# The last product's second tile in two 128-column halves, with its store cut in two

## The chip, the cores and the metric

The kernel runs on one core of one Trainium2 chip. Its time is the device time of one execution in microseconds (us); all times here are in us unless marked ns. The engines are TensorE (PE; its weight loads are shown apart as PEld), VectorE (DVE), ScalarE (ACT), GpSimd (POOL) and SyncE (SP). SP, ACT and POOL also issue DMA transfers, each on a queue of its own (SPq, ACTq, POOLq in the profile), and 16 DMA engines move the bytes.

## The reference

The inputs are `x` (8 batches, 8 heads, 512 rows, 64 columns), `state` (8 batches, 8 heads, 32 rows, 64 columns), `w_in` (512 x 2048) and `w_out` (2048 x 512), all float32.

```python
scores = scale * x @ state^T;  a  = softmax(scores);  xread = a @ state
scores2 = scale * state @ x^T; a2 = softmax(scores2); sread = a2 @ x
rows = concat([xread, sread], axis=2)      # (8, 8, 544, 64)
rows = rows.transpose(0, 2, 1, 3).reshape(8 * 544, 8 * 64)
h = rows @ w_in
out = max(0.01 * h, h) @ w_out             # (4352, 512) float32
```

So each batch gives 512 rows of `out` from `xread` and behind them 32 rows from `sread`: batch b's sread rows are rows 544 b + 512 to 544 b + 543.

## The kernel before, in words

Partitions are the 128 lanes of the on-chip memory; a tile is [partitions, columns]. The kernel works batch by batch. For a batch it computes attention, folds `state` and `w_in` into one matrix M, gets the hidden layer hT (2048 hidden units in 16 blocks of 128 partitions, 512 rows as columns) by `ff1`, and then the product with `w_out`. That product is done with seven half-size products in place of eight, Strassen's way: `product(b, n, v)` is the n-th of the seven for the row tile v (128 of 256 rows), eight matmuls which add up in one PSUM bank. The products 1, 6, 7 and 4 add up in the banks called "x", the products 2, 5 and 3 in those called "b". `after(b, n)` takes the intermediate sums out (`keep`, `y_add`) and stores them (`y_pair`). For the last batch, b = 7, the "x" sums of the two row tiles lie in a bank each (tiles `ppw`).

The order of the work on every engine is that of the program text (a manual schedule): an engine or a queue takes its instructions in that order, and each waits for what it needs. So an instruction that waits holds up all behind it on the same engine or queue.

At the start TensorE runs matmuls on an idle tile (`spin`), between the first real ones. They write to a bank that nobody reads.

The end of the program goes as follows. The sread rows of all eight batches, 256 rows, go through the two layers together: `f_product` is the first layer, `two_product(q, n)` the second, again in seven products, and `q.y` holds the result, 128 partitions by two halves u, of 512 columns each. Half u holds four batches of 32 rows. After product 3 half u = 0 is done and goes out from SP, after product 4 half u = 1 from ACT, in four stores of 64 KB each (line 1284), one per batch. Meanwhile the last batch's own products lie between: products 2, 5, 6 and 7 between the `f_product` calls, product 3 behind the sread rows, and product 4 as the last work of the program (lines 1287 to 1294):

```python
for v in range(2):
    product(b, 4, v)
    (VEC, SCA)[v](y_block(b, 1, 0)[:, v], prods[b]["x"][v])
    nc.sync.dma_start(rows_of(b)[2 + v][:, :HN], y_block(b, 1, 0)[:, v])
```

VEC is a copy on DVE, SCA one on ACT. `y_block(b, 1, 0)[:, v]` is a 128 x 256 part of a tile in SBUF (HN = 256, P = 128); `rows_of(b)[2 + v]` are every fourth row of the batch, from row 2 + v on, so that each of these two stores takes 128 rows of 1 KB. Before them, `y_pair(b, 0, HN, DM)` stores two row tiles at once (256 KB in rows of 1 KB, line 745).

After the last store SP waits for every transfer that is still under way; then all engines meet, and the program ends.

Of the kernel before, what the change touches and what calls it, by code (L numbers as in the profile page):

```python
# [9 lines left out]
P = 128  # L10
B, H, S, D = 8, 8, 512, 64
NS = 32
DFF = 2048
DM = 512
SROW = S + NS
NT = S // P
NK = H // 2
# [3 lines left out]
FP32 = mybir.dt.float32  # L21
AF = mybir.ActivationFunctionType
ALU = mybir.AluOpType
# [4 lines left out]
def kernel(  # L28
# [9 lines left out]
    nc = tc.nc  # L38

    consts = ctx.enter_context(tc.tile_pool(name="consts", bufs=1))  # L40
# [6 lines left out]
    psum = ctx.enter_context(tc.tile_pool(name="psum", bufs=2, space=bass.MemoryType.PSUM))  # L47
# [5 lines left out]
    VEC, SCA, POO = nc.vector.tensor_copy, nc.scalar.copy, nc.gpsimd.tensor_copy  # L53
# [83 lines left out]
    def cast_x0(q, copy):  # L137
        v = q % 2
        copy(
            xs[0][q // 2][:, :, 2 * v:2 * v + 2].rearrange("p t h d -> p h t d"),  # L140
            xf[q][:].rearrange("p h (t d) -> p h t d", t=NT),
        )
# [15 lines left out]
    def spin_bank():  # L158
        return psum.tile([P, S], FP32, name="pspin", tag="py")

    def spin(p, n, w=S):
        for _ in range(n):
            nc.tensor.matmul(p[:, :w], lhsT=idle[:, :P], rhs=idle[:, :w], start=True, stop=True)
# [26 lines left out]
    def st1_evict():  # L190
        SCA(
            st1[:].rearrange("p (k q r) -> p k q r", k=NK, r=4),
            pst[:, :, D:].rearrange("p r (k q) -> p k q r", q=8),
        )
# [365 lines left out]
    HN = DM // 2  # L560
# [13 lines left out]
    def w_block(r, c, j0, j1):  # L574
        return w_out_bf[:, HJ * r + j0:HJ * r + j1, HN * c:HN * (c + 1)]
# [12 lines left out]
    hTs, sums, prods = {}, {}, {}  # L588
# [20 lines left out]
    def w_of(n, j):  # L609
        if n < 4:  # L610
            r, c = {1: (0, 0), 2: (1, 0), 3: (1, 1)}[n]
            return w_block(r, c, j, j + 1)[:, 0]
        return tw[{4: 4, 5: 1, 6: 2, 7: 3}[n]][j // 4][:, j % 4]

    def product(b, n, v, j0=0, j1=8):
        q = prods.setdefault(b, {})
        bank = "x" if n in (1, 6, 7, 4) else "b"
        first = n in (1, 2, 5) and v == 0 and j0 == 0
        if first:
            if b == B - 1 and n == 1:  # L620
                ts = [psum.tile([P, 2, DM], FP32, name="ppw", tag=t, bufs=1) for t in ("sc", "big")]
                q[bank] = [t[:, 0, :HN] for t in ts]
                q["whole", bank] = None
            else:
                t = psum.tile([P, 2, HN], FP32, name=f"pp{bank}", tag="py")
                q[bank] = [t[:, u] for u in range(2)]
                q["whole", bank] = t[:]
        wide = b == B - 1 and n == 1
        q["open", bank] = first or (wide and j0 == 0)
        at = slice(P * v, P * (v + 1))  # L630
        low = slice(HN * 1 + P * v, HN * 1 + P * (v + 1))
        for j in range(j0, j1):
            lhsT = {
                1: lambda: hTs[b][:, j, at],
                2: lambda: hTs[b][:, HJ + j, at],
                4: lambda: hTs[b][:, HJ + j, low],
                3: lambda: sums[b, 4][:, j, at],
                5: lambda: sums[b, 1][:, j, at],
                6: lambda: sums[b, 2][:, j, at],
                7: lambda: sums[b, 3][:, j, at],  # L640
            }[n]()
            nc.tensor.matmul(  # L642
                q[bank][v], lhsT=lhsT, rhs=w_of(n, j), start=q["open", bank] and j == 0,
                stop=j == 7, skip_group_check=True,
            )

# [71 lines left out]
    def keep(b, n):  # L718
        q = prods[b]
        if n == 5:  # L720
            t = consts.tile([P, 2, HN], FP32, name="s5", tag="stf4")
        else:
            t = ypool.tile([P, 2, HN], FP32, name=f"s{n}", tag=f"s{n}", bufs=1)
        q[n] = t
        for to, of in bank_parts(q, "b" if n == 5 else "x", t[:]):
            SCA(to, of)

    def y_block(b, u, c):
        q = prods[b]
        if ("y", u) not in q:  # L730
            q["y", u] = ypool.tile([P, 2, DM], FP32, name="ysb", tag="ysb")
        return q["y", u][:, :, HN * c:HN * (c + 1)]

    def y_add(b, u, c, bank, n):
        q = prods[b]
        kept = q[n][:]
        for v, (to, of) in enumerate(bank_parts(q, bank, y_block(b, u, c))):
            in1 = kept if q["whole", bank] is not None else kept[:, v]
            nc.vector.tensor_tensor(out=to, in0=of, in1=in1, op=ALU.add)  # L739
# [4 lines left out]
    def y_pair(b, u, c0=0, c1=DM):  # L744
        nc.sync.dma_start(
            pair_rows(b, u)[:, :, c0:c1],
            prods[b]["y", u][:, :, c0:c1],
        )

    def after(b, n):  # L750
        if n == 1:
            keep(b, 1)
        elif n == 2:
            y_add(b, 0, 0, "b", 1)
        elif n == 6:
            keep(b, 6)
        elif n == 5:
            keep(b, 5)
        elif n == 7:
            y_add(b, 1, 1, "x", 5)  # L760
        elif n == 3:
            y_add(b, 0, 1, "b", 6)
            y_pair(b, 0)
        elif n == 4:
            SCA(y_block(b, 1, 0), prods[b]["whole", "x"])
            y_pair(b, 1)

    def rows_of(b):
        return out[b * SROW:b * SROW + S, :].rearrange("(p t) f -> t p f", t=NT)
# [11 lines left out]
    def x0_t(q):  # L781
        ps = psum.tile([P, NT, P], FP32, name="pxth", tag=("ph", "py")[q // 2])
        for t in range(NT):
            nc.tensor.matmul(
                ps[:, t, :], lhsT=pair_of(a0, t, q), rhs=ident[:], start=True, stop=True
            )
        SCA(a0.xT[:, :, q, :], ps[:])
# [3 lines left out]
    def scores0(q):  # L791
        if q < 2:
            if q == 0:
                sct["low"] = psum.tile([P, 2, NT, 2, NS], FP32, name="sct", tag="sc", bufs=1)
            sct[q] = sct["low"][:, q]
        else:
            t = psum.tile([P, NT, 2, NS], FP32, name="sct", tag=("big", "py")[q - 2], bufs=q - 1)
            sct[q] = t[:]
        for t in range(NT):
            nc.tensor.matmul(  # L800
                sct[q][:, t].rearrange("p c n -> p (c n)"),
                lhsT=a0.xT[:, t, q, :], rhs=stbd[:, q].rearrange("p g n -> p (g n)"),
                start=True, stop=True,
            )

    scn, e10, r0, qb0 = {}, {}, {}, {}
# [82 lines left out]
    for q in range(2):  # L889
        cast_x0(q, VEC)  # L890
        x0_t(q)
        if q == 0:
            st1_evict()
            bank = spin_bank()
            spin(bank, 3, S // 2)
    spin(bank, 2, S // 2)
    scores0(0)
    cast_x0(2, VEC)
    x0_t(2)
    spin(bank, 2, S // 2)  # L900
    scores0(1)
    cast_x0(3, VEC)
    x0_t(3)
    bank = spin_bank()
# [3 lines left out]
    scores0(2)  # L908
    max0(2)
    rows0(0)  # L910
    spin(bank, 2, S // 2)
    scores0(3)
    max0(3)
    spread0(scn[0], m, False)
# [5 lines left out]
    q = [recip0(0)]  # L920
# [331 lines left out]
    b = B - 1  # L1252
    for c in range(2):
        f = f_open(c)
        for n, own in (
            (1, ()), (2, ((2, 5)[c], 0)), (6, ()), (5, ((2, 5)[c], 1)),
            (7, ()), (3, ((6, 7)[c], 0)), (4, ((6, 7)[c], 1)),
        ):
            f_product(f, n)
            if own:  # L1260
                product(b, *own)
                if own[1]:
                    after(b, own[0])
            if c == 0 and n == 2:
                for m in (1, 2):
                    s_sum(b, m, 4, 8, nc.vector)
                for j in range(0, HJ, 2):
                    s_sum(b, 4, j, j + 2, nc.gpsimd)
        if c == 0:
            y_pair(b, 0, 0, HN)  # L1270
            q = two_open(hs, 0, None, "ph")
            for n in range(1, 5):
                two_sum(q, n, 0, 4, nc.vector)
# [4 lines left out]
    for n in (1, 2, 6, 5, 7, 3, 4):  # L1278
        two_product(q, n)
        if n in (3, 4):  # L1280
            u = n - 3
            for v in range(NK):
                r0 = (NK * u + v) * SROW + S
                (nc.sync, nc.scalar)[u].dma_start(
                    out[r0:r0 + NS, :], q.y[NS * v:NS * (v + 1), u]
                )
    for v in range(2):
        product(b, 3, v)
    y_add(b, 0, 1, "b", 6)
    y_pair(b, 0, HN, DM)  # L1290
    for v in range(2):
        product(b, 4, v)
        (VEC, SCA)[v](y_block(b, 1, 0)[:, v], prods[b]["x"][v])
        nc.sync.dma_start(rows_of(b)[2 + v][:, :HN], y_block(b, 1, 0)[:, v])


# [28 lines left out]
```

## Time and profile before

| what | us |
|---|---|
| median of three runs (lowest, highest) | 202.45 (202.29, 202.52) |
| the profiled execution | 202.64 |
| its span, first to last instruction | 200.9 |
| TensorE busy | 193.9 (97% of the span) |
| DVE, ACT, POOL busy | 158.7, 142.0, 72.9 |
| granted TensorE clock, mean over the span | 0.997 of full speed |
| bytes moved by DMA | 27.75 MB, 138 GB/s on the mean |

The profile is of one execution. Its views that are used here: the chain of work that ended last (followed back from the last instruction, at each step to what released it); the timeline (instructions in order of time, each with its start, its length, the engine, the line, and in brackets the engine's idle time before it with what ended it); the answers for one line (shortest, median and longest duration, first and last start, and for a DMA the time from issue to landing); and windows (busy time of each engine in a stretch, the granted clock, the mean busy share of the 16 DMA engines and the GB/s they moved). "out<-in" names tiles; `x16` counts instructions. Releasers are inferred from the times of events, so two events that fall together can be taken for each other.

### The profile page before, as it was taken

Reading aid. Unit: us, or ns where it says so; the run is one execution under the profiler, and the core shown is the slowest. Engines: PE = TensorE matmul, PEld = TensorE weight load, DVE = VectorE, ACT = ScalarE, POOL = GpSimd, SP = SyncE. Lnnn points to the kernel's source line nnn. Section 1 sums busy time; section 2 is a strip of 40 time slices with the busy share of each in tenths; the row PEclk is TensorE's granted clock in tenths of the full one; section 3 lists DMA queues with packets and bytes.
Section 4 is the critical chain, followed back from the end, with each engine's and each line's share of the span. In section 5 each row is a group of like instructions: output and inputs, shape, how many; then the busy total and the mean of one; then the engine's idle time right before and its main releaser. Section 6 shows DMA issues by size and latency. Waiting matters only on the chain.

```text
span 200.9 us, 4601 instructions
## 1 busy us (share of the span) xinstructions
PE 193.9 (97%) x1853; PEld 130.2 (65%) x1880; DVE 158.7 (79%) x241; ACT 142.0 (71%) x274; POOL 72.9 (36%) x76
## 2 busy tenths in 40 slices
PE   7899999999999999999999999999999999999993
PEld 3653444343476767776776677676767777799982
DVE  2665798589999989985999889898999945984712
ACT  3679747999889868766877779777868555757420
POOL 8834173991091373037300760054004600540000
PEclk9999999999999999999999999999999999999998
DMA  5999999697999844952473404220025202210115
GB/s 191 202 206 291 217 274 176 124 337 170 204 222 223 312 45 37 277 211 55 90 223 144 123 18 89 104 109 0 0 107 157 53 3 104 108 50 7 52 39 170
DMA packets 38773, 27.75 MB, mean 138 GB/s; under 512 B 24416, under 2 KB 35808, under 8 KB 38752
## 3 DMA queue, kind: packets, MB, share of 16 engines
q1 hardware_dynamic: 33584, 20.78, 39.9%
q0 software_dynamic: 4832, 6.29, 15.5%
q10 hardware_dynamic: 336, 0.39, 0.8%
q8 instruction: 14, 0.23, 0.5%
q14 instruction: 7, 0.06, 0.1%
HBM read 17.30 MB, written 8.91 MB: 131 GB/s over the span
## 4 chain that ended last, share of the span: by engine, by line
PE 77%; DMA 16%; POOL 3%; ACT 2%; issue 1%; ACTq 1%; SPq 0%; POOLq 0%
PE ph L442 21%; PE ppx L642 18%; PE ppb L642 15%; DMA xl<-in_x_dram 7%; DMA w_out_bf<-in_moe_w_out_dram 6%; PE ppr L699 6%; PE py L547 3%; PE pm L421 3%; PE pf L520 3%; PE ppw L642 3%; PE psr L394 2%; POOL w_in_bf L145 2%; DMA st_t<-stb 1%; DMA out_dram<-ysb 1%; PE sc L256 1%
## 5 line engine op out<-in xcount | busy, mean ns | idle before, releaser
L447 ACT ACTIVATE hT<-ph 128x512 bf16<-128x512 f32 x112 | 66.5, 604 | 25.1 <-PE ph L442 22.0
L607 POOL TENSOR_TENSOR S<-hT,S 128x512 bf16<-128x512 bf16 x24 | 32.1, 1358 | 82.2 <-DVE S L607 55.5
L442 PE MATMUL ph<-aT,M 128*128 128x512 bf16 x202 | 60.7, 379 | 0.1
L642 PEld LDWEIGHTS <-S 128*128 128x128 bf16 x384 | 37.0, 98 | 12.7 <-issue 0.9
L642 PEld LDWEIGHTS <-hT 128*128 128x128 bf16 x288 | 28.0, 98 | 11.1
L607 DVE TENSOR_TENSOR S<-hT 128x1024 bf16<-128x1024 bf16 x24 | 25.0, 1069 | 3.4 <-ACT hT L447 3.3
L442 PEld LDWEIGHTS <-M 128*128 128x128 bf16 x224 | 20.9, 98 | 8.7 <-issue 2.7
L642 PE MATMUL ppx<-tw,S 128*128 128x256 bf16 x160 | 20.8, 273 | 0.3
L547 PEld LDWEIGHTS <-hT 128*128 128x128 bf16 x96 | 9.1, 98 | 11.4 <-issue 1.0
L547 PE MATMUL py<-w_out_bf,hT 128*128 128x512 bf16 x61 | 15.6, 379 | 0.1
L739 DVE TENSOR_TENSOR ysb<-ppb,s 128x512 f32<-128x512 f32 x12 | 8.3, 692 | 6.2 <-PE ppb L642 6.2
L642 PE MATMUL ppb<-w_out_bf,hT 128*128 128x256 bf16 x96 | 12.4, 273 | 0.2
L642 PE MATMUL ppb<-tw,S 128*128 128x256 bf16 x96 | 12.4, 273 | 0.1
L642 PE MATMUL ppb<-w_out_bf,S 128*128 128x256 bf16 x96 | 12.3, 273 | 0.2
L435 ACT CAST M<-pm 128x1024 bf16<-128x1024 f32 x11 | 11.2, 1018 | 0.5 <-PE pm L421 0.5
L642 PE MATMUL ppx<-w_out_bf,hT 128*128 128x256 bf16 x80 | 11.2, 272 | 0.1
L347 ACT ACTIVATE e<-sc,mcol 128x512 bf16<-128x512 f32 x16 | 11.1, 701 | 0.0
L586 POOL TENSOR_TENSOR tw<-w_out_bf 128x512 bf16<-128x512 bf16 x8 | 9.0, 1154 | 4.5 <-DMA w_out_bf<-in_moe_w_out_dram 4.5
L642 PE MATMUL ppx<-tw,hT 128*128 128x256 bf16 x80 | 10.4, 273 | 0.2
L341 DVE TENSOR_REDUCE mcol<-sc 128x2 f32<-128x1024 f32 x8 | 9.7, 1214 | 0.0
L266 DVE TRANSPOSE_TENSOR_REDUCE mrow<-sc 128x32 f32<-128x1024 f32 x7 | 8.7, 1241 | 1.2 <-PE sc L256 1.2
L289 DVE TRANSPOSE_TENSOR_REDUCE r<-e 128x32 f32<-128x1024 bf16 x7 | 8.7, 1244 | 1.1 <-ACT e L330 0.8
(148 smaller groups left out, 323.7 us busy)
## 6 DMA issues: line engine op xcount, KB each, us to landing
out_dram<-ysb SPq DMA_DIRECT2D x11, 512.0 KB, 2.6
xl<-in_x_dram SPq DMA_DIRECT2D x5, 1024.0 KB, 6.0
out_dram<-ysb SPq DMA_DIRECT2D x9, 256.0 KB, 4.5
w_in_bf<-in_moe_w_in_dram POOLq DMA_DIRECT2D x4, 512.0 KB, 9.6
xf<-in_x_dram SPq DMA_DIRECT2D x4, 256.0 KB, 4.0
w_out_bf<-in_moe_w_out_dram POOLq DMA_DIRECT2D x4, 256.0 KB, 14.1
x<-in_x_dram POOLq DMA_DIRECT2D x2, 512.0 KB, 14.1
w_out_bf<-in_moe_w_out_dram POOLq DMA_DIRECT2D x2, 512.0 KB, 16.0
```

The costliest lines, as they stand in the source:

```text
L266: nc.vector.tensor_reduce(out=m1[:], in_=flat.rearrange("p (c j) -> p c j", j=NS), axis=AX.X, op=ALU.max, apply_transpose=True,)
L289: nc.vector.tensor_reduce(out=r1[:], in_=e1[:].rearrange("p (c j) -> p c j", j=NS), axis=AX.X, op=ALU.add, apply_transpose=True,)
L341: nc.vector.tensor_reduce(out=a.m2[:], in_=a.sc[:], axis=AX.X, op=ALU.max, negate=True)
L347: nc.scalar.activation(out=a.e2[:, g], in_=a.sc[:, g, :], func=AF.Exp, bias=a.m2[:, g:g + 1], accum_out=a.r2[:, g:g + 1],)
L435: copy(a.M[:, :, cols], pm[:])
L442: nc.tensor.matmul(ph[:], lhsT=a.M[:, g, P * j:P * (j + 1)], rhs=a.aT[:, g, :], start=(g == 0), stop=(g == 1),)
L447: nc.scalar.activation(out=hT[:, j, :], in_=ph[:], func=AF.Prelu, scale=1 / SCALE, alpha=0.01)
L547: nc.tensor.matmul(y.py, lhsT=hT[:, j, P * i:P * (i + 1)], rhs=w_out_bf[:, j, :], start=(j == 0), stop=(j == 15),)
L586: eng.tensor_tensor(out=tw[n][u][:, at], in0=in0, in1=in1, op=ALU.subtract)
L607: eng.tensor_tensor(out=part(n), in0=in0, in1=in1, op=op)
L642: nc.tensor.matmul(q[bank][v], lhsT=lhsT, rhs=w_of(n, j), start=q["open", bank] and j == 0, stop=j == 7, skip_group_check=True,)
L699: nc.tensor.matmul(q.bank[w], lhsT=lhsT, rhs=w_of(n, j), start=n in (1, 2, 5) and j == 0, stop=j == HJ - 1, skip_group_check=True,)
```

## The change

There are four edits.

- The second row tile of product 4 is done in two halves of 128 columns: the first 128 columns in its bank as before, the other 128 in a fresh bank (`end`). As the fresh bank lacks the sum of products 1, 6 and 7, these 128 columns are copied by ACT into a tile `last` after product 7, and DVE adds them at the end. ACT copies the first half and stores it (64 KB) from its own queue; DVE's half is stored (64 KB) from SP.
- `product` gets the columns c0 to c1 and a bank to write to.
- The sread rows of half u = 0 go out in three stores in place of four: batches 0 and 1 alone (64 KB each), batches 2 and 3 together (128 KB). The target of the third is a block of two batches by 32 rows, with a stride of 544 rows between the batches; its source is 64 partitions.
- Of the spins between the first matmuls, nine of 256 columns become four of 512 and one of 256, at the same places.

```diff
-    def product(b, n, v, j0=0, j1=8):
+    def product(b, n, v, j0=0, j1=8, c0=0, c1=HN, bank_of=None):
...
             nc.tensor.matmul(
-                q[bank][v], lhsT=lhsT, rhs=w_of(n, j), start=q["open", bank] and j == 0,
+                q[bank][v][:, c0:c1] if bank_of is None else bank_of,
+                lhsT=lhsT, rhs=w_of(n, j)[:, c0:c1],
+                start=(q["open", bank] or bank_of is not None) and j == 0,
                 stop=j == 7, skip_group_check=True,
             )
...
             bank = spin_bank()
-            spin(bank, 3, S // 2)
-    spin(bank, 2, S // 2)
+            spin(bank, 1)
+            spin(bank, 1, S // 2)
+    spin(bank, 1)
...
-    spin(bank, 2, S // 2)
+    spin(bank, 1)
     scores0(1)
...
-    spin(bank, 2, S // 2)
+    spin(bank, 1)
     scores0(3)
...
                 if own[1]:
                     after(b, own[0])
+                if own == (7, 1):
+                    last = consts.tile([P, P], FP32, name="last", tag="stf2")
+                    SCA(last[:], prods[b]["x"][1][:, P:])
...
             u = n - 3
-            for v in range(NK):
-                r0 = (NK * u + v) * SROW + S
-                (nc.sync, nc.scalar)[u].dma_start(
-                    out[r0:r0 + NS, :], q.y[NS * v:NS * (v + 1), u]
-                )
+            rows = out.rearrange("(b s) f -> b s f", s=SROW)[NK * u:NK * (u + 1), S:]
+            for v0, v1 in ((0, 1), (1, 2), (2, 4)) if u == 0 else ((v, v + 1) for v in range(NK)):
+                (nc.sync, nc.scalar)[u].dma_start(rows[v0:v1], q.y[NS * v0:NS * v1, u])
...
-    for v in range(2):
-        product(b, 4, v)
-        (VEC, SCA)[v](y_block(b, 1, 0)[:, v], prods[b]["x"][v])
-        nc.sync.dma_start(rows_of(b)[2 + v][:, :HN], y_block(b, 1, 0)[:, v])
+    y = y_block(b, 1, 0)
+    product(b, 4, 0)
+    VEC(y[:, 0], prods[b]["x"][0])
+    nc.sync.dma_start(rows_of(b)[2][:, :HN], y[:, 0])
+    end = psum.tile([P, P], FP32, name="end", tag="ph")
+    product(b, 4, 1, c1=P)
+    SCA(y[:, 1, :P], prods[b]["x"][1][:, :P])
+    nc.scalar.dma_start(rows_of(b)[3][:, :P], y[:, 1, :P])
+    product(b, 4, 1, c0=P, bank_of=end[:])
+    nc.vector.tensor_tensor(out=y[:, 1, P:], in0=end[:], in1=last[:], op=ALU.add)
+    nc.sync.dma_start(rows_of(b)[3][:, P:HN], y[:, 1, P:])
```

## The prediction

> **What bounds the kernel now.** I read the page's chain first, then the chain of the last stretch in order of time, then that stretch's timeline, and last the DMA views of the same stretch.
>
> ```profile
> span 200.9 us, 4601 instructions
> ...
> PE 77%; DMA 16%; POOL 3%; ACT 2%; issue 1%; ACTq 1%; SPq 0%; POOLq 0%
> ```
>
> TensorE carries the span from some 39 us on. The edits lie where it does not: in the first 9 us and behind its last products.
>
> ```profile
> 194.19 0.02 issue
> 194.21 0.38 ACT ysb L706
> ...
> 196.04 1.68 DMA out_dram<-ysb
> 197.72 0.35 ACT ysb L1293
> ```
>
> This chain, taken from 190 us on, says that ACT's last copy (L1293) was released by a store. It was not: as built, that copy waits for TensorE alone, and the store's landing fell 0.02 us beside TensorE's end. The timeline shows it:
>
> ```profile
> 193.79 1.76 SPq L1284 DMA_DIRECT2D out_dram<-ysb  x4
> ...
> 194.61 1.88 ACTq L1284 DMA_DIRECT2D out_dram<-ysb  x4
> ...
> 195.76 1.91 PE L642 MATMUL ppw<-tw,hT 128*128 128x256 bf16 x16
> 195.96 0.69 DVE L739 TENSOR_TENSOR ysb<-ppb,s 128x512 f32<-128x512 f32 x1 [2.19 <-PE ppb L642]
> 196.68 0.39 SPq L745 DMA_DIRECT2D out_dram<-ysb  x1
> 196.83 0.42 DVE L1293 COPY ysb<-ppw 128x256 f32<-128x256 f32 x1 [0.18 <-PE ppw L642]
> 197.28 1.16 SPq L1294 DMA_DIRECT2D out_dram<-ysb  x2
> 197.70 0.37 ACT L1293 COPY ysb<-ppw 128x256 f32<-128x256 f32 x1 [3.12 <-DMA out_dram<-ysb]
> ```
>
> TensorE ends at 195.76 + 1.91 = 197.67, ACT's copy at 198.07, the last issue starts at 198.10. Next, what the stores of lines 1294 and 1284 take from issue to landing:
>
> ```profile
> L1294 SPq DMA_DIRECT2D out_dram<-ysb x2: 345/350/356, 197.3 to 198.1; - x2
> ...
> DMA to landing us min/median/max: 1.8/2.0/2.2
> ```
>
> ```profile
> L1284 SPq DMA_DIRECT2D out_dram<-ysb x4: 350/414/432, 193.8 to 195.1; - x4
> L1284 ACTq DMA_DIRECT2D out_dram<-ysb x4: 395/444/473, 194.6 to 196.0; - x4
> ...
> DMA to landing us min/median/max: 1.6/1.8/2.1
> ```
>
> The last store took 1.84 (the minimum of its line): 199.94. The remaining 0.93 of the span is closing work, unchanged. Last, four windows: the sread stores; the final stores; one 256 KB store in rows of 1 KB alone; one 512 KB store in rows of 4 KB alone.
>
> ```profile
> 194.60:197.45 2.85, 2.85 (x29) 2.51 (x26) 1.12 (x2) 0.00 (x0) 0.00 (x0) 1.00 0.70 184
> 197.50:199.50 2.00, 0.17 (x2) 0.00 (x0) 0.00 (x0) 0.37 (x1) 0.00 (x0) 1.00 0.74 262
> 189.40:190.40 1.00, 1.00 (x11) 0.89 (x10) 0.93 (x3) 0.00 (x0) 0.00 (x0) 1.00 0.76 262
> 86.05:87.52 1.47, 1.47 (x13) 1.12 (x12) 0.72 (x2) 0.99 (x2) 0.00 (x0) 1.00 0.86 357
> ```
>
> The last two columns are the busy share of 16 DMA engines and GB/s. One engine's rate is GB/s over 16 times the share: 1 KB rows 262 / (16 x 0.756) = 21.7 KB per us (the DMA view of that window has 75.6%), 4 KB rows 357 / (16 x 0.861) = 25.9, and 2 KB rows with two queues at work 184 / (16 x 0.70) = 16.4, which counts overlapping rows twice. For 2 KB rows I take 23.8, midway between the first two.
>
> **The change, part by part.** The sum is against the profiled execution: 202.64, of which 200.87 is span; the median of the three runs is 202.45, so 0.19 goes off at the end.
>
> *Warm-up spins.* Nine 256-column matmuls become four of 512 and one of 256: 2304 columns either way, the same weights, the same places in the order. At nothing: up to 39 us the chain runs over DMA loads (34.9% and 31.9% of it are two loads), and TensorE idles 0.55 at 6.87 for a cast. Without that cover it would be four instructions less, a gain of hundredths.
>
> *The kept half (`last`).* One ACT copy of 128 columns, 0.27 by the one such row (L191, 271 ns). It waits for DVE's L739 add, 188.10 + 0.42 = 188.52; behind it ACT's next copy (L704) is due at 188.97, after 1.00 idle. It ends near 188.82, so at nothing. Without 0.15 of that room L704 would slip, whose reader on DVE starts at 189.90, 0.56 after L704 ends.
>
> *The split.* Eight matmuls of 256 columns (0.87) become 16 of 128, which the profile has at 0.89 for 16 (L520): TensorE ends 0.02 later, at 197.69. The fresh bank's last reader, DVE's L709 add, ended at 193.77, so TensorE does not wait. The first half ends near 197.24; ACT copies it (0.27) and issues its own store at 197.57, with nothing behind it on that queue; by the ACT issues of 1.7 to 2.0 it lands by 199.6. The second half ends in a DVE add of 128 columns: 0.69 for 512 and 0.42 for 256 give 0.29. Issue at 197.69 + 0.03 + 0.29 + 0.03 = 198.04, against 198.10: -0.06. Then 64 KB instead of 128 KB: the 64 KB stores took 1.6 to 2.1, the 128 KB one 1.84; for a store with the engines to itself I take 1.7, -0.14. Together -0.20; from 0 (landing like their median) to -0.30.
>
> *The sread store of two batches.* SP issues three stores instead of four; the third takes 64 rows of 2 KB, and as built its target is two blocks of 32 rows, outermost count 2, from 64 partitions. It saves one issue of 0.43 on SP, worth nothing: SP then waits until 196.65 for DVE's 0.69 add anyway. If the issue itself is dearer than its neighbours' 0.35 to 0.43, there is room from 194.67 to 196.65. No wait of the stores behind it names this store; only the closing wait does.
>
> What it costs on the DMA engines the trace doesn't show: every store in it has 32 or 128 outermost rows, a multiple of 16, and runs on all 16 engines. The bounds are 16 engines (nothing) and as many as the outermost count gives equal shares to, two. I take two: the rows fit equal shares of the outermost count, and no row shows a block of a count below 16 being cut further. Then two engines get 32 rows each, 65.5 KB, and all later stores have their share on these engines too. Their work from the first row on, at 194.67 + 0.88 = 195.55 (the lone 256 KB store, issued 188.55, shows its first row near 189.45):
> - 65.5 KB at 23.8: 2.75
> - ACT's four sread stores, 4.1 KB each per engine: 16.4 / 23.8 = 0.69
> - the 256 KB store of L745: 16.4 / 21.7 = 0.76
> - the 128 KB store: 8.2 / 21.7 = 0.38
> - the two halves, 4.1 KB each; rows of 512 B aren't priced here, at 21.7: 0.38
>
> Sum 4.96. Each queue has the next store ready before the engine runs dry, so the order doesn't matter: the last row passes at 200.51, and the landing follows 0.35 later (the lone store: last row 190.3, landing 188.55 + 2.13). 200.86 against 199.94: **+0.92**. This contains the split's end, whose 0.20 is lost behind the two engines. With all at 25.9: 4.43, +0.4. With ACT's rows and as many of the long store's at the 16.4 of the shared window, 0.62 more and a landing lag of 0.48: +1.65.
>
> [...]
>
> **Rivals.**
>
> *The store is spread over 16 engines.* Its place is the third SP issue. For it: every store shown keeps 16 engines busy. Against it: none of them has an outermost count below 32. Then only the split is left: 202.45 - 0.20 = 202.25, within what a measurement tells from no change. The point from which this decides: between 195.55 and the last row of the shortened end, 199.2, an engine has 3.65, of which 2.21 is other work; 1.44 is left, against 5.5 over the number of engines: from four engines on the store is hidden.
>
> *The rows of two queues slow each other on the two engines.* For it: 16.4 in the shared window. Against it: that share counts overlapping rows twice, and the eight stores landed in 1.6 to 2.1. Then +1.65, 204.1.
>
> *The split gives more, and the store is spread.* A landing at 1.4 and an earlier issue would give -0.5, 201.95. No store in the profile landed in under 1.6.
>
> **How the numbers follow.** Two engines as summed: 0.79. Two engines, slowed by both queues: 0.08. Spread over 16: 0.11. Spread, with a larger gain: 0.02. The time is that of the likeliest: 202.45 + 0.92 = 203.37. Its own range is +0.4 to +1.3; with the slowed case the range is 202.8 to 204.1, and the spread cases, 0.13, are left out. Differences under 0.2% (0.4 us) can't be told from none here: faster 0.02, same 0.11, slower 0.87.
>
> **What would show it.** The third SP sread store should land some 4 us after its issue, against 1.9; SP's closing wait should end near 200.9; from 197.6 on the mean DMA share should fall to an eighth (two of 16) in a long stretch before the end, where it was near 1. TensorE should end at 197.69 and the last issue stand at 198.04. If the final stores land by 199.8 at a full DMA share, the store was spread and the forecast is wrong. If TensorE's end itself has moved by more than 0.1, something earlier has changed that I costed at nothing.

## The result, and the profile after

| what | before | after |
|---|---|---|
| median on the same chip (lowest, highest), six runs each | 202.50 (202.29, 202.85) | 205.75 (205.28, 206.84) |
| the profiled execution | 202.64 | 205.30 |
| start of the last product (first `ppw` matmul of the tail) | 195.76 | 195.88 |
| start of the last issue | 198.10 | 199.22 |
| last landing | 199.94 | 202.34 |
| end of the span | 200.87 | 203.27 |

The ratio is 1.0168, with a 95% interval of 1.0144 to 1.0192: 3.25 us slower, where 0.92 was forecast and 204.1 was the upper end of the range. The direction held, the size did not.

The page of the changed kernel begins its chain as follows (shares of the span):

```profile
span 203.3 us, 4640 instructions
...
PE 78%; DMA 15%; POOL 2%; SPq 1%; ACT 1%; issue 0%; DVE 0%; POOLq 0%
```

Its chain of the last stretch, in order of time (start, length, what):

```profile
194.30 1.75 PE ppb L642 x16
196.05 1.32 PE ppw L642 x16
197.37 0.46 PE end L642 x8
197.83 0.02 issue
197.85 0.29 DVE ysb L1304
```

The chain stops at 198.14, and the span ends at 203.27. What fills the last five microseconds is no engine's work, so this view can't say; the timeline and the answers for the lines can. The timeline of the changed kernel:

```profile
193.91 1.56 SPq L1290 DMA_DIRECT2D out_dram<-ysb  x3
...
194.74 2.00 ACTq L1290 DMA_DIRECT2D out_dram<-ysb  x4
...
195.88 1.48 PE L642 MATMUL ppw<-tw,hT 128*128 128x256 bf16 x16
196.08 0.69 DVE L741 TENSOR_TENSOR ysb<-ppb,s 128x512 f32<-128x512 f32 x1 [2.20 <-PE ppb L642]
196.80 0.39 SPq L747 DMA_DIRECT2D out_dram<-ysb  x1
...
197.20 0.61 PE L642 MATMUL end<-tw,hT 128*128 128x128 bf16 x8
...
197.41 1.72 SPq L1298 DMA_DIRECT2D out_dram<-ysb  x1
197.70 1.16 ACTq L1302 DMA_DIRECT2D out_dram<-ysb  x1
197.85 0.29 DVE L1304 TENSOR_TENSOR ysb<-end,last 128x128 f32<-128x128 f32 x1 [0.47 <-PE end L642]
199.22 0.57 SPq L1305 DMA_DIRECT2D out_dram<-ysb  x1
```

TensorE ends at 197.81 and DVE's add at 198.14, both as forecast (0.12 later, because this execution reached its last product 0.12 later). But the issue of the store before (L1298) now holds SP for 1.72 us, where the two issues of L1294 took 0.345 and 0.356, and the last store starts 1.08 us after its data is ready (198.14 to 199.22). The last store, by the answer for its line (an issue of 566 ns):

```profile
L1305 SPq DMA_DIRECT2D out_dram<-ysb x1: 566/566/566, 199.2 to 199.2; - x1
...
DMA to landing us min/median/max: 3.1/3.1/3.1
```

It lands 3.12 after its issue, against 1.84 for the last store before. The records have the end of a store as landings on its semaphore, a counter that SP's closing waits look at. In the kernel before, each of the twelve stores from 188 us on has sixteen, as many as there are DMA engines (those of the last one at 199.83 to 199.94). The merged store (the third of SP's three at L1290) was issued at 194.78. The records of its semaphore show a single event at 195.85 and two late landings only, at 200.57 and 200.61, 5.8 us after the issue. I read that as two engines, and both late. Five windows (the last two columns are the mean busy share of 16 DMA engines and GB/s):

```profile
194.60:197.45 2.85, 2.85 (x35) 2.63 (x33) 1.12 (x2) 0.16 (x2) 0.00 (x0) 1.00 0.41 99
197.50:199.50 2.00, 0.31 (x6) 0.14 (x3) 0.29 (x1) 0.17 (x1) 0.00 (x0) 1.00 0.66 154
199.50:200.50 1.00, 0.00 (x0) 0.00 (x0) 0.00 (x0) 0.00 (x0) 0.00 (x0) 1.00 0.91 299
200.50:201.50 1.00, 0.00 (x0) 0.00 (x0) 0.00 (x0) 0.00 (x0) 0.00 (x0) 1.00 0.42 137
201.50:202.34 0.84, 0.00 (x0) 0.00 (x0) 0.00 (x0) 0.00 (x0) 0.00 (x0) 1.00 0.06 18
```

Before, the first two of these had shares of 0.70 and 0.74. Now the engines idle while TensorE still works (0.41) and are busy after it is done (0.91): the rows of the other fourteen engines, too, were held back. The bare tail of two engines, which was to show as a long share of an eighth, is only the last microsecond.

### The profile page after: what moved, and what is told of

Read it like the earlier page. It is cut to its first block, busy times and chain, and to the rows that moved or that the text cites. A ratio compares the mean times of both kernels' runs of the same rounds, so it can differ in the third digit from the quotient of the medians.

```text
span 203.3 us, 4640 instructions
## 1 busy us (share of the span) xinstructions
PE 195.4 (96%) x1884; PEld 129.8 (64%) x1884; DVE 159.4 (78%) x242; ACT 142.3 (70%) x275; POOL 72.3 (36%) x76
## 3 DMA queue, kind: packets, MB, share of 16 engines
q0 software_dynamic: 4832, 6.29, 15.3%
## 4 chain that ended last, share of the span: by engine, by line
PE 78%; DMA 15%; POOL 2%; SPq 1%; ACT 1%; issue 0%; DVE 0%; POOLq 0%
PE ph L442 23%; PE ppx L642 17%; PE ppb L642 15%; DMA xl<-in_x_dram 7%; DMA w_out_bf<-in_moe_w_out_dram 6%; PE ppr L701 6%; PE py L547 3%; PE pm L421 3%; PE ppw L642 3%; PE pf L520 3%; PE psr L394 2%; DMA st_t<-stb 2%; POOL w_in_bf L145 2%; PE sc L256 1%; SPq L240 1%; ACT xb L126 1%
## 5 line engine op out<-in xcount | busy, mean ns | idle before, releaser
L442 PE MATMUL ph<-aT,M 128*128 128x512 bf16 x224 | 65.3, 379 | 0.0
```

The source lines that it names most:

```text
L442: nc.tensor.matmul(ph[:], lhsT=a.M[:, g, P * j:P * (j + 1)], rhs=a.aT[:, g, :], start=(g == 0), stop=(g == 1),)
```

## The experiments

The kernels were compared with the kernel before on the same chip; its medians there were 202.24 to 202.35. "Above" means above that median.

**The parts one by one.** The changed kernel with four sread stores in place of three, that is the spins and the split alone:

```diff
-            rows = out.rearrange("(b s) f -> b s f", s=SROW)[NK * u:NK * (u + 1), S:]
-            for v0, v1 in ((0, 1), (1, 2), (2, 4)) if u == 0 else ((v, v + 1) for v in range(NK)):
-                (nc.sync, nc.scalar)[u].dma_start(rows[v0:v1], q.y[NS * v0:NS * v1, u])
+            for v in range(NK):
+                r0 = (NK * u + v) * SROW + S
+                (nc.sync, nc.scalar)[u].dma_start(
+                    out[r0:r0 + NS, :], q.y[NS * v:NS * (v + 1), u]
+                )
```

> The changed kernel with four sread stores on SP as before; the split and the spins stay. Theory 'merged store': all of the loss is that store, so this runs at 202.1 to 202.5 (ratio to before 0.998 to 1.000), every sread store lands within 2.2 us of its issue, and the last issue stands some 0.06 earlier behind TensorE's end than before. Rival 'split': the halves, the fresh bank or the extra store on ACT's queue cost part of the 3.2 us; then this stays above 203.

Measured: 203.86 against 202.35, ratio 1.0079 (1.0056 to 1.0102). 1.51 of the 3.25 stay without the merged store, though the split was to gain. The timeline of this kernel shows an end at which no issue is held:

```profile
196.43 1.48 PE L642 MATMUL ppw<-tw,hT 128*128 128x256 bf16 x16
...
197.96 0.36 SPq L1300 DMA_DIRECT2D out_dram<-ysb  x1
198.25 0.36 ACTq L1304 DMA_DIRECT2D out_dram<-ysb  x1
198.40 0.29 DVE L1306 TENSOR_TENSOR ysb<-end,last 128x128 f32<-128x128 f32 x1 [0.47 <-PE end L642]
198.72 0.34 SPq L1307 DMA_DIRECT2D out_dram<-ysb  x1
```

From the first matmul of the last product to the last issue it takes 2.29, against 198.10 - 195.76 = 2.34 before: 0.05, where 0.06 was forecast. But the 64 KB landed 1.85 after the issue, where the 128 KB had taken 1.84. In this profile the split gains 0.04 and no more. And from the last landing (200.57) to the end of the span it takes 1.33, against 0.93.

The kernel before with the merged store alone:

```diff
-            for v in range(NK):
-                r0 = (NK * u + v) * SROW + S
-                (nc.sync, nc.scalar)[u].dma_start(
-                    out[r0:r0 + NS, :], q.y[NS * v:NS * (v + 1), u]
-                )
+            rows = out.rearrange("(b s) f -> b s f", s=SROW)[NK * u:NK * (u + 1), S:]
+            for v0, v1 in ((0, 1), (1, 2), (2, 4)) if u == 0 else ((v, v + 1) for v in range(NK)):
+                (nc.sync, nc.scalar)[u].dma_start(rows[v0:v1], q.y[NS * v0:NS * v1, u])
```

> The kernel before with nothing but batches 2 and 3 of the sread rows in one store. Theory 'merged store': 205.0 to 206.2, the store lands 5 to 6 us after its issue, and the closing wait ends near 202. Rival 'split': under 203.4, and the rest comes with the split.

Measured: 204.90 against 202.35, ratio 1.0127 (1.0098 to 1.0156): 2.55 above, where the forecast for it and the split together was 0.92 (205.0 to 206.2 was expected here). The merged store's semaphore has its two landings 5.8 and 6.0 after the issue. The issues of the last product's stores are held here too (line L1292: 0.55 and 1.70 us).

The kernel before with the spins alone (its edit is below), and with the split alone (the changed kernel with the old spins and four sread stores):

```diff
-            spin(bank, 3, S // 2)
-    spin(bank, 2, S // 2)
+            spin(bank, 1)
+            spin(bank, 1, S // 2)
+    spin(bank, 1)
...
-    spin(bank, 2, S // 2)
+    spin(bank, 1)
```

> The kernel before with nothing but the spin edit. With four sread stores but split and spins (the first experiment) 1.5 us were lost, while TensorE's last work ended 0.6 later already at 189 us; the state's transposes landed late (4.41 us after their issue, against 2.82). Theory 'spins': the edit moves the first microseconds and with them the transposes, so this alone costs 0.5 to 1.2 (202.9 to 203.6). Rival 'chance': the place of the transposes varies from execution to execution whatever the spins, so this stays within 0.4 of before.

> The kernel before with nothing but the split (old spins, four stores on SP). Theory 'closing order': the last store now has the semaphore that SP's closing waits look at first, with seven waits of 0.06 behind it, 0.43; the split itself gains 0.05; so this runs at +0.3 to +0.5 over before, and from the last landing to the end of the span 1.33 us pass instead of 0.93. If 'spins' is wrong too, +1.2 or more.

Measured: the spins 203.15 against 202.25, ratio 1.0048 (1.003 to 1.0066), 0.90 above; the split 203.31, ratio 1.0056 (1.004 to 1.0072), 1.06 above. Neither was worth nothing, and the split lost more than the 0.3 to 0.5 expected of it. Spins and merged store together make 3.45, near the 3.25 of the whole. I do not add the split's own loss, because its end lies behind the two engines there; that is argued from the traces, no kernel shows it.

**Why the merged store is dearer than summed.** The changed kernel without ACT's four sread stores (the sread rows of batches 4 to 7 are left out):

```diff
-            for v0, v1 in ((0, 1), (1, 2), (2, 4)) if u == 0 else ((v, v + 1) for v in range(NK)):
+            for v0, v1 in ((0, 1), (1, 2), (2, 4)) if u == 0 else ():
```

> The changed kernel without ACT's four sread stores (the sread rows of batches 4 to 7 are not written). In the changed kernel the merged store's rows pass slowly in its first 2 us, while ACT's stores are in flight, and ACT's rows take 0.2 to 0.4 us each. Theory 'two queues on two engines': alone, 32 rows per engine pass at 84 ns each from the first on, the store lands at most 4.2 us after its issue (in the changed kernel 5.82), and the end comes 1.5 to 2.2 us earlier than in the changed kernel (the slow start 1.5, and 0.7 of rows left out). Rival 'the store is slow by itself', from how its rows are described: it still lands after 5.3 us or more, and the end comes at most 0.8 earlier.

Measured: 205.94, one execution, span 203.26; the time is no lower than the changed kernel's, so I go by the landings. Without any row of the second queue the merged store still landed 5.89 after its issue, and the last landing came at 202.10, only 0.24 earlier than in the changed kernel. So it is not the two queues that slow each other. The DMA view of this kernel from 196.05 to 197.70 (queue q1 is SP's):

```profile
DMA packets 22, 0.05 MB, mean 27 GB/s; under 512 B 0, under 2 KB 0, under 8 KB 22
...
q1 hardware_dynamic: 22, 0.05, 11.8%
```

In 1.65 us two engines (11.8% of sixteen is 1.9) moved 22 rows of 2 KB, and there was nothing else to move. The records of the packets give the rest: the first row starts at 196.09; eleven are done by 197.24, and single rows of this start take up to 0.45 and 0.52 us; from then on one engine takes a row every 0.08 us, the other one now and then needs 0.2 to 0.4 for a row, and the last row ends at 200.37. So 4.28 us for 65.5 KB on the later engine, 15.3 KB per us, where a steady row every 0.08 us would be 25.6. The other engine landed 0.63 earlier (200.07 against 200.70). The end of this kernel is the tail that I had looked for:

```profile
200.50:202.10 1.60, 0.00 (x0) 0.00 (x0) 0.00 (x0) 0.00 (x0) 0.00 (x0) 0.91 0.13 40
```

0.13 is two engines of sixteen.

Two merged stores of two batches each, and one of four (one execution each):

```diff
-            for v0, v1 in ((0, 1), (1, 2), (2, 4)) if u == 0 else ((v, v + 1) for v in range(NK)):
+            for v0, v1 in ((0, 2), (2, 4)) if u == 0 else ((v, v + 1) for v in range(NK)):
```

```diff
-            for v0, v1 in ((0, 1), (1, 2), (2, 4)) if u == 0 else ((v, v + 1) for v in range(NK)):
+            for v0, v1 in ((0, 4),) if u == 0 else ((v, v + 1) for v in range(NK)):
```

> The changed kernel with batches 0 and 1 in such a store as well, two merged stores behind each other. Theory 'two engines': both go to the same two engines, which get 64 rows each in place of 36, 28 x 84 ns = 2.4 us more; the start is 0.4 to 0.9 earlier, so the end comes 1.3 to 2.2 us later than in the changed kernel. Rival 'a fixed price of such a store' (its issue, one slow start): within 0.7 us of the changed kernel, and rival 'other engines for each store': no later than the changed kernel.

> The changed kernel with all four batches of u = 0 in one store, outermost count 4, 128 rows, issued 0.87 earlier than the two-batch store. Theory 'per engine': it runs on four engines with 32 rows each, each row at some 135 ns, so it lands about 5.8 to 6.3 after its issue, and the end comes 0.5 to 1.0 earlier than in the changed kernel (203.3 of span). Rival 'per transfer' (its rows are described one after the other, whatever the engines): twice the rows, 9 to 11 us to landing, and the end 3 us later or more. Rival 'two engines in any case': 64 rows each, the end 3.5 to 4 later, as with two merged stores.

Measured: 209.03 (span 207.25) and 205.84 (span 204.06). In the first, the rows of the two stores take from 195.31 to 204.17, 4.43 for each on the later engine, with rows of other stores between them; the second store landed at 202.56 and 204.50, behind the first (199.66 and 199.81), which I read as the same two engines for both. The 4.0 us over the changed kernel's span is more than I had expected, and the timeline says how the time reaches the end:

```profile
197.95 0.29 DVE L1304 TENSOR_TENSOR ysb<-end,last 128x128 f32<-128x128 f32 x1 [0.47 <-PE end L642]
199.43 0.27 ACT L1301 COPY ysb<-ppw 128x128 f32<-128x128 f32 x1 [4.62 <-DMA out_dram<-ysb]
199.88 0.54 ACTq L1302 DMA_DIRECT2D out_dram<-ysb  x1
204.56 0.34 SPq L1305 DMA_DIRECT2D out_dram<-ysb  x1
```

The last store's data is ready at 198.24, and it is issued at 204.56. In the kernels before and after, the records from 188 us on show the stores of SP and ACT on eight semaphores in turn (100, 102, 105, 106, 107, 116, 117, 118), and ahead of the last store a wait on its own semaphore (in the changed kernel on 118 at 199.17, the issue at 199.22). Here the last store's semaphore is that of the second merged store (117, landings at 202.56 and 204.50), and the issue follows 0.06 after the second of them. In the changed kernel the merged store's semaphore (100) has no later user, so it had no such wait.

In the second kernel the store of four batches has four late landings, at 199.95, 199.98, 200.30 and 200.94: as many as batches, so 32 rows for each. They come 5.5 to 6.5 after the issue (194.44), against 5.8 for the store of two, so here the price goes with the 32 rows behind one late landing and hardly with the bytes of the store. The end, though, came 0.8 later than in the changed kernel (spans 204.06 and 203.27), where 0.5 to 1.0 earlier was expected. The reason is the same wait as above: the last store uses the semaphore of the store of four.

```profile
198.38 0.29 DVE L1304 TENSOR_TENSOR ysb<-end,last 128x128 f32<-128x128 f32 x1 [0.47 <-PE end L642]
...
201.00 0.34 SPq L1305 DMA_DIRECT2D out_dram<-ysb  x1
```

Its data is ready at 198.67, the store of four lands at 200.94, and the last store is issued at 201.00.

The changed kernel with the merged store on POOL's queue, which the profile lists as `software_dynamic` where SP's and ACT's are `hardware_dynamic`:

```diff
-                (nc.sync, nc.scalar)[u].dma_start(rows[v0:v1], q.y[NS * v0:NS * v1, u])
+                (nc.gpsimd if v1 - v0 > 1 else (nc.sync, nc.scalar)[u]).dma_start(
+                    rows[v0:v1], q.y[NS * v0:NS * v1, u]
+                )
```

> The changed kernel with its two-batch store issued on POOL's software queue in place of SP's hardware queue. Theory (the shape of the store fixes two engines, whatever queue describes it): its rows again take some 4.3 us on few engines, the last landing stays later than 201.5 us and the time is 204.8 to 206.5. Rival (the two engines are a property of the hardware queue's split): the rows go to 16 engines, the store lands within 3 us of its first row, the last landing is near 200.6 and the time 203.4 to 204.2, as with four stores (203.86).

Measured: 204.96 (one execution, span 203.19), last landing 202.21. The DMA issues of this kernel around 194.1 (KB each, us from issue to landing):

```profile
out_dram<-ysb POOLq DMA_DIRECT2D x1, 128.0 KB, 6.4
```

The records have sixteen landings of this store: fourteen at 196.41 to 196.75 and two at 200.41 and 200.50. Its rows went as 32 packets of 4 KB, sixteen for each of the two late landings, from 195.64 to 200.04: 4.4 us again, again with single packets of 0.7 and 0.9 us in the first two microseconds. Both the two engines and their slowness go with the shape of the store on both queues. That the later issues are held is also the same (L1300: 1.41).

**What the split lost.** SP's closing waits look at the eight semaphores in the same order in the kernels before and after (100 first, 118 last), and each takes 0.06 when there is nothing left to wait for (198.56, 198.62, 198.69, 198.75 in the kernel before). In the kernel before, the last store is on the one looked at last. With one store more the last store is on the one looked at first, and seven waits stand behind its landing: 200.58, 200.65, 200.71, ... 201.01 in the spins-and-split kernel. The kernel before with one sread store cut into two of 16 rows shows this alone:

```diff
-                (nc.sync, nc.scalar)[u].dma_start(
-                    out[r0:r0 + NS, :], q.y[NS * v:NS * (v + 1), u]
-                )
+                for r in ((0, 16), (16, 32)) if (u, v) == (0, 0) else ((0, 32),):
+                    (nc.sync, nc.scalar)[u].dma_start(
+                        out[r0 + r[0]:r0 + r[1], :], q.y[NS * v + r[0]:NS * v + r[1], u]
+                    )
```

> The kernel before with one of the 64 KB sread stores cut into two of 16 rows, so that the last store gets the first semaphore of the closing list; nothing else differs. Theory 'closing order': +0.35 to +0.5, all of it between the last landing and the end of the span (1.33 instead of 0.93). Rival 'split': without the split nothing changes, within 0.2.

Measured: 202.72 against 202.25, ratio 1.0024 (1.0014 to 1.0034), 0.47 above. From the last landing (199.48) to the end of the span it takes 1.35, against 0.93.

That leaves some 0.6 of the split's 1.06. In the profile of the split alone (203.88, the longest of its five times), an instruction fetch falls into the last product; the DMA view of that kernel from 196.2 to 196.4, and its timeline:

```profile
q8 instruction: 1, 0.02, 48.3%
```

```profile
197.13 1.09 SPq L1299 DMA_DIRECT2D out_dram<-ysb  x1
197.42 0.79 ACTq L1303 DMA_DIRECT2D out_dram<-ysb  x1
197.57 0.29 DVE L1305 TENSOR_TENSOR ysb<-end,last 128x128 f32<-128x128 f32 x1 [0.47 <-PE end L642]
198.31 0.40 SPq L1306 DMA_DIRECT2D out_dram<-ysb  x1
```

To take the closing waits away and leave the rest, one sread store was moved to POOL's queue, so that the last store is again on the semaphore looked at last:

```diff
-                (nc.sync, nc.scalar)[u].dma_start(
+                (nc.gpsimd if u == v == 0 else (nc.sync, nc.scalar)[u]).dma_start(
```

> The kernel before with the split of the last product alone (old spins, four sread stores), and the first of the four sread stores issued on POOL's software queue, so that eleven stores are left on the hardware queues and the last store falls on the semaphore that is waited for last, as in the kernel before. Theory (the split alone took +1.06 because of seven closing waits behind its store, 0.43, and of an instruction fetch at 196.3 us that held the end's issues, some 0.6): the close after the last landing falls from 1.34 to 0.9 us, the fetch and the longer issues beside it (1.09 and 0.79 us for the stores of the last product) stay, time 0.4 to 0.75 us above the kernel before. Rival (the closing order was all that held the split back): time 0.05 to 0.25 us below the kernel before, that is 202.0 to 202.2.

Measured: 202.58 against 202.24, ratio 1.002 (1.0006 to 1.0034). The close is back at 0.93 and 0.7 of the 1.06 is gone, but the split is still no gain. The fetch is there (195.62), and three of ACT's sread stores land 2.9 to 3.5 after their issue, against 1.7 to 2.0; the long issues that I expected are not (0.47 and 0.36). The profiled execution (202.16) is the shortest of twelve, so it does not show what costs the median 0.34. So the closing order is shown.

For the remainder the landings say more than the views. In both profiles one landing of the sixteen is late, from the fifth or sixth sread store on: in the split alone the store issued at 194.90 has fifteen landings by 196.83 and the last at 199.02; with the store on POOL, the one issued at 194.42 has fifteen by 196.21 and the last at 197.90. The records give the fetch as one packet of 16 KB, under way for 1.55 and 1.25 us. Of the last store, too, one landing is late: 200.64 against 200.11 for the other fifteen, and 199.46 against 199.24. In the kernel before its landings lie within 0.11. The spins-and-split kernel has eight TensorE instructions less than the split alone; its fetch comes at 202.89, behind its end, its last store's landings lie within 0.21, and it is 0.61 above the spins alone (1.51 - 0.90) where the split alone cost 1.06. All this speaks for the fetch, by way of one late engine, as the remainder. It is not shown: the two late ends are single executions, and no kernel took the fetch out of the tail while keeping the old spins.

**What the spins cost.** The chain of the stretch from 28 us, in the spins-only kernel and then in one that follows below:

```profile
33.79 1.23 SPq L240
...
35.13 4.32 DMA st_t<-stb
39.45 0.04 issue
39.49 0.41 PE sc L256 x8
```

In the kernel before, that transposing load of the state took 2.82 in the same place:

```profile
36.19 2.82 DMA st_t<-stb
39.01 0.04 issue
39.05 0.41 PE sc L256 x8
```

The DMA view of the spins-only kernel from 35.0 to 35.6 has an instruction fetch within the transposes:

```profile
q1 hardware_dynamic: 420, 0.11, 123.4%
q8 instruction: 1, 0.02, 9.2%
...
st_t<-stb SPq DMA_TRANSPOSE x1, 4.3
```

In the kernel before, the third fetch comes at 32.94, ahead of `st_t` and of most of the transposes' packets. Four spin matmuls less, with a weight load each (the profiles have 1880 weight loads before and 1884 after, eight more by the split and four less by the spins), are eight TensorE instructions less, so I supposed that they move the fetch. Two kernels test that. Each has the columns and places of the new spins and nine matmuls' worth of instructions: one cuts each spin of 512 columns into 448 and 64, the other leaves them and cuts four spins of the first group in two. Their edits against the kernel with the spins alone:

```diff
-            spin(bank, 1)
+            spin(bank, 1, 448)
+            spin(bank, 1, 64)
```

```diff
-    spin(spin_bank(), 7)
+    first = spin_bank()
+    spin(first, 3)
+    spin(first, 8, S // 2)
```

> The kernel before with its spins as in the change, except that each spin of 512 columns is issued as one of 448 and one of 64. Columns (2304) and places are those of both kernels; the number of matmuls is nine again, as before. Theory (four matmuls less move TensorE's later instruction fetches, and one of these then meets the transposing load of the state): the third instruction fetch goes back from 35.0-36.4 to 32.5-32.9 us, st_t lands 2.8 to 2.9 us after its issue in place of 3.7 to 4.4, and the time is that of the kernel before, within 0.25 us. Rival (the wider matmuls themselves, or the order of the first 9 us, cost it): fetch times aside, the time stays 0.7 to 1.0 us above the kernel before, as with the spin edit alone (+0.90).

> The kernel before with the spins as in the change (five instead of nine matmuls), and four matmuls added elsewhere: of the seven spins of 512 columns at the very start, four are cut into two of 256 each. Theory (the number of TensorE instructions ahead of the transposes sets where the fetch falls): third fetch at 32.5-32.9 us, st_t lands 2.8 to 2.9 us after its issue, time within 0.25 us of the kernel before. Rival (wide spins between the first transposes cost it): the time stays 0.7 to 1.0 us above the kernel before.

Measured: 202.25 against 202.26, ratio 0.9997 (0.9987 to 1.0006), and 202.37, ratio 0.9999 (0.9983 to 1.0016). Third fetch at 32.93 and 32.85. The chain of the second one:

```profile
34.24 1.24 SPq L240
...
35.59 3.17 DMA st_t<-stb
38.76 0.04 issue
38.80 0.41 PE sc L256 x8
```

Neither the width of the spins nor their place matters; the number of TensorE instructions ahead of the transposes does. In the first kernel st_t took 2.9, in the second 3.2, a little more than I expected of it. It is so in all fourteen profiles of this case: with nine matmuls' worth of instructions (seven profiles) the third fetch is at 32.5 to 32.9, st_t lands 2.8 to 3.2 after its issue and the last product starts at 195.1 to 195.8; with five (seven profiles) the fetch is at 35.0 to 36.4, st_t takes 3.5 to 4.4 and the last product starts at 195.8 to 196.4. What carries this to the end is the landing of `st_t`: from it to the start of the last product 156.75 to 156.80 pass in thirteen of the fourteen (156.94 in the kernel with the merged store on POOL). The instruction count is shown as the cause; that the fetch is what slows the transposes is read from their meeting. An 8 KB fetch of another queue (35.8 to 37.4) falls among them in all fourteen, so a fetch as such does not explain the difference.

No kernel beat the kernel before.

## Why the prediction was wrong, step by step

- **Warm-up spins, "at nothing": wrong, 0.90.** The cover that I named (loads up to 39 us) was the path that they lengthened, through the instruction count and not through TensorE's time. The prediction named the sign of it, TensorE's end moved by more than 0.1: it came at 197.81 in place of 197.69. In the two profiled executions the difference is only 0.12, because that of the kernel before started its last product at 195.76, the latest of the seven with nine matmuls. So the forecast of +0.92 stands against 2.66 in the profiles, of which 0.12 is this step, and against 3.25 in the medians.
- **The kept half, at nothing: right.** The copy ran 188.68 to 188.95, and ACT's next at 189.10 was due then.
- **The split, -0.20: wrong; its own gain was 0.04, and alone it lost 1.06.** TensorE's end (197.81 - 0.12 = 197.69) and the earlier issue (0.05) were right where nothing held the issue. The 1.7 for the landing was a choice between 1.6 and 2.1 that assumed bytes matter: 64 KB in rows of 512 B took 1.85 in the spins-and-split kernel, 128 KB in rows of 1 KB 1.84 before. What I did not look at is that one store more changes which closing wait stands last (+0.43 alone); in the changed kernel the store saved by the merging takes that back.
- **The merged store on two engines: right; its price was mis-sized.** The term that failed is "65.5 KB at 23.8: 2.75". That rate came from stores spread over sixteen engines; on the later of this store's two engines it was 15.3, 4.28, in the kernel without ACT's stores. The rows that ran steadily did go at 25.6, a little above the 23.8; what the term lacks is the slow start and the slow rows between. The other missed term is the first row at 195.55, which came at 196.07 (0.12 for the later execution, 0.3 for an issue of 0.70 in place of 0.4, 0.1 left open). The sum by its own steps, with the row times of the changed kernel: its 2 KB rows from 196.07 to 200.27, ACT's rows in between and in the gaps; 0.76 + 0.38 + 0.38 for the three last stores, 201.79; 0.35 to the landing, 202.14. Measured 202.34. The other terms held.
- **"Each queue has the next store ready", "there is room for a dearer issue": wrong where it was not tested.** The issue of the merged store itself fitted (0.70), but the issues behind it did not: 1.72 on SP, 1.16 on ACT. The last store was therefore late for all sixteen engines, which is why the share was 0.91 at 200 and not an eighth. It did not set the end: fourteen of its landings were in by 201.69, and the two late ones came at 202.06 and 202.34, behind rows that follow each other without a gap up to 202.02. Without ACT's sread stores the last store's own issue took 1.51. What holds such an issue the profile does not name. Beside the one late landing of the split alone issues took 1.09 and 0.79, beside that of the split with a store on POOL 0.47 and 0.36. That lagging engines hold the issues is my reading, not shown.
- **The rivals.** Sixteen engines: fallen, by the landings: 2 late ones for two batches, 4 for four, 2 on POOL's queue, where each of the last twelve stores of the kernel before has sixteen. The two engines of the forecast were a choice between two bounds that no store of the kernel before shows; what shows them are these landings and the share of 0.13 at the end without ACT's stores. The records have events and not counts: on SP's queue a single event 1.07 after the merged store's issue, then the two late ones; on POOL's queue sixteen. What the single event stands for they don't say. Two queues slowing each other: the nearest in time (204.1), but not the mechanism, since the store was as slow without the second queue; its nearness is chance. A larger gain of the split: fallen.

## What to carry to other kernels

A store merged over an outer stride is not one store less: here it had one late landing per batch (2 for two, 4 for four), where the last twelve stores of the kernel before have sixteen within 0.52 us, and the last of them came 5.8 to 6.5 after its issue in the kernels with one such store, where the 64 KB stores of the kernel before took 1.6 to 2.1. Price its rows by a row of that shape or leave the range open upwards, because the issues of the stores behind it can be held as well (up to 1.72 here). At the end of a kernel, count the stores too: here one store more put the last one on another semaphore, with seven closing waits behind it, 0.43 us. And when dummy matmuls are added or removed, ask where the instruction fetches move to; here the same columns in four matmuls and four weight loads more or less were worth 0.9 us.

## What the runs showed of the hardware that I had not expected

- The later of two engines took 4.1 to 4.4 us for 32 rows of 2 KB, on SP's queue as on POOL's; on SP's the first five or six rows of each took 1.15 in the kernel without ACT's stores. Why these start so slowly is open.
- On POOL's queue the merged store has sixteen landings, fourteen of them within 0.34 us (196.41 to 196.75) while most of the store's packets were still to come (195.64 to 200.04), two 4 us later.
- Stores behind the slow one took up to 1.7 us to issue, on the other queue as well (1.16 on ACT; with the store of four batches up to 1.92 there, 4.07 for ACT's four sread issues).
- An instruction fetch of 16 KB among transposing loads goes with 3.5 to 4.4 us for such a load, in place of 2.8 to 3.2. Among the last stores it goes with one late landing of sixteen, up to 2.2 us behind the others.
